# Top-32 search over 56 candidates in place of four full passes, with a per-row proof and a fallback branch

## The chip, the cores and the metric

The kernel runs on one core of one Trainium2 chip. The metric is the device time of one execution in microseconds. An execution consists of the span, from the first to the last instruction of the program, and of a little under 2 us around it. The numbers of the trace come from one profiled execution of the kernel before.

## The reference

Three layers stand behind one another. The first is an attention that keeps, in each row of 576 scores, those that are at least as large as the 32nd largest. The other two are a feed-forward layer and a mixture of eight experts.

```python
batch, n_heads, seq, head_dim = (4, 8, 576, 64)
scores = scale * np.matmul(q, k.transpose(0, 1, 3, 2))
kth = np.partition(scores, -32, axis=-1)[..., -32:-31]
scores = np.where(scores >= kth, scores, -1000000000.0)
scores = scores - np.max(scores, axis=-1, keepdims=True)
attn = np.exp(scores)
attn = attn / (np.sum(attn, axis=-1, keepdims=True) + 1e-09)
x = np.matmul(attn, v)                    # to 2304 tokens x 512
h = np.maximum(x @ w_in, 0.0)             # 512 x 2048
x = h * h @ w_out                         # 2048 x 512
# then a softplus-noise gate picks 2 of 8 experts for a token; an expert is
# relu(x @ w1[e]) @ w2[e] with 512 x 1024 and 1024 x 512
```

The attention has 4 x 8 x 576 = 18432 rows of scores, and each needs its largest score and its 32nd largest.

## The kernel before, in words

**Units.** A unit is a pair of heads and 128 query rows. Four full units of 128 rows and one unit of left-over rows cover the 576 rows of a pair; in the left-over unit the 64 last rows of two heads share the 128 partitions. So there are 144 tiles of 128 x 576 scores, two in a full unit and one in a left-over one.

**One tile.** `scores` (L342) lets TensorE multiply q (split in two parts for precision, L314) by k into `ps`, ScalarE copies `ps` to `sb` (L350), and VectorE searches: four times `max` gives the eight largest of what is left (L355), and three times `match_replace` writes a very small number over these eight (L357). The four groups of eight stand in `m`; the first is the row's largest, the last the 32nd. `softmax` (L361) lets GpSimd multiply the two by constants into `bs` (L363), ScalarE make a large penalty for scores below the 32nd (L364), GpSimd subtract it (L365), and ScalarE take the exponential with the row sum (L366). TensorE then transposes the tile (L376), ScalarE copies it (L378), GpSimd and TensorE handle the last 64 keys (L397 to L406), TensorE multiplies by v (L413), and VectorE divides by the row sum (L385, L389).

**The rest.** The feed-forward layer takes chunks of three token tiles as soon as all heads of these tokens are done; its matmuls stand at L266 to L268 and L280 to L282, its activations at L286 to L290. Before it can run, its weights are converted once from 64-bit to 32-bit numbers and split (`convert`, L134 to L151); two such conversions go with each unit, so they fall into the first part of the span. `route` (L162) picks the experts and scatters tokens to `xs`. The experts (L499) follow at the end. A last part that handles experts with more than 640 tokens stands behind a branch (L833, L834), which these inputs do not take.

**What sets the order.** Each engine runs its own queue in order. The program hands the units out in a fixed interleaving: unit i+2 starts while unit i-1 is finished, and between their steps `step` (L577) puts a fixed allowance of feed-forward work (`RATE`, `FILLS`), at lower priority. A planner then orders the instructions of every engine by priority and by readiness in its own model of the times, and adds the waits. VectorE's queue therefore holds instructions of two or three searches in turn, and everything small that VectorE does for the conversions and for `route`.

**Storage that the change touches.** `vt` holds v of a batch in five tiles of eight buffers (L330), `sb` has eight buffers, `w` four, `m` and `bs` six each.

The search before:

```python
src = sb
for i in range(4):
    nc.vector.max(m[:, i, :], src)
    if i < 3:
        nc.vector.match_replace(out=w, in_to_replace=m[:, i, :], in_values=src, imm_value=NEG)
        src = w
```

Of the kernel before, what the change touches and what calls it, by code (L numbers as in the profile page):

```python
# [8 lines left out]
F32 = mybir.dt.float32  # L9
F32R = mybir.dt.float32r  # L10
I32 = mybir.dt.int32
U32 = mybir.dt.uint32
BF16 = mybir.dt.bfloat16
AF = mybir.ActivationFunctionType
ALU = mybir.AluOpType
PSUM = bass.MemoryType.PSUM

P = 128
SHAPE = (4, 8, 576, 64)
EPS = 1e-9  # L20
BIG = 2.0 ** 96
NEG = -3.0e38
# [19 lines left out]
def tile_order():  # L42

    B, _, S, _ = SHAPE
    n = S // P
    tiles = []
    for b in range(0, B, 2):
        tiles += [(b, i) for i in range(n)] + [(b + 1, i) for i in range(n)] + [(b, None)]
    return tiles


@with_exitstack
def attention_ffn_moe(ctx: ExitStack, tc: tile.TileContext, q, k, v, w_ffn, w_route, noise, w_exp, out):
    nc = tc.nc
    B, H, S, D = SHAPE
    NT, DM = out.shape
    DFF = w_ffn.shape[0] * P
    E, F = w_exp.shape[0], w_exp.shape[1] * P
    NTT = NT // P
    NF = DFF // P  # L60
# [5 lines left out]
    SCALE = 1.0 / float(D) ** 0.5  # L66
# [5 lines left out]
    ROW = DM + 4  # L72


    wsc = [nc.dram_tensor(f"wsc{f}", (P, 2, 2, DM), F32, kind="Internal").ap() for f in range(NF)]
    xs = nc.dram_tensor("xs", (E * NT, ROW), F32, kind="Internal").ap()


    cpool = ctx.enter_context(tc.tile_pool(name="cpool", bufs=1))
# [11 lines left out]
    nc.vector.tensor_scalar(base, iota_e, float(NT), None, op0=ALU.mult)  # L91
    onesb = cpool.tile([P, P], BF16, name="onesb")
    nc.gpsimd.memset(onesb, 1.0)
    cb = cpool.tile([P, 2], F32, name="cb")
    nc.gpsimd.memset(cb[:, 0:1], -SCALE)
    nc.gpsimd.memset(cb[:, 1:2], BIG)
    tiles = tile_order()
    tok_i = cpool.tile([P, NTT], I32, name="tok_i")
    for t, (b, i) in enumerate(tiles):
# [10 lines left out]
    fpool = ctx.enter_context(tc.tile_pool(name="fpool", bufs=2))  # L110
# [194 lines left out]
    apool = actx.enter_context(tc.tile_pool(name="apool", bufs=2))  # L305
# [2 lines left out]

    K4 = {}
    V = {}  # L310

    def split(eng, hi, lo, src, top):

# [13 lines left out]
    def prep_v(b):  # L327
        V[b] = []
        for c in range(NFULL + 1):
            vt = apool.tile([P, H, D], F32, name="vt", bufs=8)  # L330
            nc.sync.dma_start(vt.rearrange("p h d -> p (h d)"), v[b, c])
            V[b].append(vt)

# [8 lines left out]
    def scores(pairs):  # L342

        ps = ps_s.tile([P, 2, 512], F32, name="ps")
        for i, (st, kt) in enumerate(pairs):
            for n in range(2):
                nc.tensor.matmul(ps[:, n, 0:HS], st, kt[:, n * HS:(n + 1) * HS],  # L347
                                 start=(i == 0), stop=(i == len(pairs) - 1))
        sb = apool.tile([P, S], F32, name="sb", bufs=8)
        nc.scalar.activation(sb.rearrange("p (n s) -> p n s", n=2), ps[:, :, 0:HS], AF.Copy)  # L350
        m = apool.tile([P, 4, 8], F32, name="m", bufs=6)
        w = apool.tile([P, S], F32, name="w", bufs=4)
        src = sb
        for i in range(4):
            nc.vector.max(m[:, i, :], src)  # L355
# [3 lines that stand above are left out]
        return sb, w, m  # L359

    def softmax(sb, w, m, sm):  # L361
        bs = apool.tile([P, 2], F32, name="bs", bufs=6)
        nc.gpsimd.tensor_tensor(bs, m.rearrange("p a b -> p (a b)")[:, 0:32:31], cb, op=ALU.mult)  # L363
        nc.scalar.activation(w, sb, AF.Relu, bias=bs[:, 1:2], scale=-BIG)  # L364
        nc.gpsimd.tensor_tensor(sb, sb, w, op=ALU.subtract)  # L365
        nc.scalar.activation(sb, sb, AF.Exp, bias=bs[:, 0:1], scale=SCALE, accum_out=sm)  # L366

    def recip(sm):
        with tc.high_priority(SOON):
# [38 lines left out]
    def times_v(b, hA, pts, t5):  # L408
        av = ps_a.tile([P, 512], F32, name="pa")
        for c in range(NFULL + 1):  # L410
            for i in range(2):
                rhs = pts[i][:, c * P:(c + 1) * P] if c < NFULL else t5[:, 0, :]
                nc.tensor.matmul(av[i * D:(i + 1) * D, 0:P], V[b][c][:, hA + i, :], rhs,  # L413
                                 start=(c == 0), stop=(c == NFULL))
# [219 lines left out]
    chunks, t = [], 0  # L634
# [105 lines left out]
    ps_m = ctx.enter_context(tc.tile_pool(name="ps_m", bufs=2, space=PSUM))  # L740
# [7 lines left out]
        background.append([expert(e, PARTS[:1], ahead), 0])  # L748
    step(10 ** 6)

    todo_e = [(e, PARTS) for e in range(E)]
    for e in range(EARLY):
        todo_e[e] = (e, PARTS[1:])
# [38 lines left out]
    def beyond(e, row):  # L792
        inside = opool.tile([P, 1], F32, name="inside")
        nc.vector.tensor_tensor(inside, row, base[:, e:e + 1], op=ALU.is_lt)
        nc.vector.tensor_scalar(inside, inside, float(-E * NT), float(E * NT), op0=ALU.mult, op1=ALU.add)
        at = opool.tile([P, 1], I32, name="at")
        nc.vector.tensor_tensor(at, inside, row, op=ALU.add)
        nc.vector.tensor_scalar(row, row, float(P), None, op0=ALU.add)
        xr = mpool.tile([P, ROW], F32, name="mr", bufs=3)
        nc.gpsimd.memset(xr, 0.0)  # L800
        nc.vector.tensor_copy(xr[:, DM + 3:DM + 4].bitcast(I32), far)
        nc.gpsimd.indirect_dma_start(
            out=xr, out_offset=None, in_=xs, in_offset=bass.IndirectOffsetOnAxis(ap=at, axis=0),
            bounds_check=E * NT - 1, oob_is_err=False)
        gi = opool.tile([P, 4], F32, name="gi")
        gate(gi, xr, e)
        cu = mpool.tile([P, DM], F32, name="cur", bufs=6)
        nc.gpsimd.memset(cu, 0.0)
        token = bass.IndirectOffsetOnAxis(ap=gi[:, 3:4].bitcast(I32), axis=0)
        nc.gpsimd.indirect_dma_start(out=cu, out_offset=None, in_=out, in_offset=token,  # L810
                                     bounds_check=NT - 1, oob_is_err=False)
        pt = ps_m.tile([P, DM], F32, name="ph")
        for c in range(NC):
            nc.tensor.transpose(pt[:, c * P:(c + 1) * P], xr[:, c * P:(c + 1) * P], ident)
        xt = opool.tile([P, NC, P], F32, name="xto")
        nc.scalar.copy(xt, pt.rearrange("p (c s) -> p c s", c=NC))
        acc = ps_acc.tile([P, DM], F32, name="acc")
        for f in range(NFE):
            raw = mpool.tile([P, 2, DM], F32, name="raww", bufs=3)
            nc.sync.dma_start(raw, w_exp[e, f])  # L820
            ph = ps_m.tile([P, DM], F32, name="ph")
            for c in range(NC):
                nc.tensor.matmul(ph[:, 0:P], raw[:, 0, c * P:(c + 1) * P], xt[:, c, :],
                                 start=(c == 0), stop=(c == NC - 1))
            ht = opool.tile([P, P], F32, name="hto")
            nc.scalar.activation(ht, ph[:, 0:P], AF.Relu)
            nc.tensor.matmul(acc, ht, raw[:, 1, :], start=(f == 0), stop=(f == NFE - 1))
        y = mpool.tile([P, DM], F32, name="y", bufs=3)
        nc.vector.scalar_tensor_tensor(y, acc, gi[:, 2:3], cu, op0=ALU.mult, op1=ALU.add)
        nc.gpsimd.indirect_dma_start(out=out, out_offset=token, in_=y, in_offset=None,  # L830
                                     bounds_check=NT - 1, oob_is_err=False)

    any_extra = nc.values_load(extra[0:1, E:E + 1], min_val=0, max_val=NT)  # L833
    with tc.If(any_extra > 0):  # L834
        none = mpool.tile([P, ROW], F32, name="mr", bufs=3)
        nc.gpsimd.memset(none, 0.0)
        nc.vector.tensor_copy(none[:, DM + 3:DM + 4].bitcast(I32), far)
        row = opool.tile([P, 1], F32, name="row")
        for e in range(E):
            nc.vector.tensor_scalar(row, first, float(e * NT), None, op0=ALU.add)  # L840
            with tc.For_i(0, (NT - CAP) // P, 1):
                blank(e, row, none)
        for e in range(E):
            nc.vector.tensor_scalar(row, first, float(e * NT), None, op0=ALU.add)
            n_extra = nc.values_load(extra[0:1, e:e + 1], min_val=0, max_val=(NT - CAP + P - 1) // P)
            with tc.For_i(0, n_extra, 1):
                beyond(e, row)


def build(shapes):  # L850
    import concourse.bacc as bacc

    nc = bacc.Bacc("TRN2", target_bir_lowering=False, num_devices=1)
    args = []
    for name, (shape, dt) in shapes.items():
        ap = nc.dram_tensor(name, shape, dt, kind="ExternalInput").ap()
        args.append(ap.bitcast(U32) if dt == mybir.dt.uint64 else ap)
    args.append(nc.dram_tensor("out", (2304, 512), F32, kind="ExternalOutput").ap())
    with tile.TileContext(nc, schedule_with_timeline_sim=True) as tc:
        attention_ffn_moe(tc, *args)  # L860
    return nc


# [57 lines left out]
```

## Time and profile before

| | us |
|---|---|
| runs | 1433.07, 1436.71, 1438.79 |
| median | 1436.71 |
| profiled execution | 1438.54 |
| its span | 1436.8 |
| TensorE matmul busy | 1278.8 |
| VectorE busy | 1028.2 |
| ScalarE busy | 844.5 |
| GpSimd busy | 819.5 |

The mean granted clock of TensorE is 0.943 of full speed. Busy time counts an instruction from its start to its end, and consecutive instructions overlap: on TensorE and VectorE the next one starts before the one ahead has ended, so a share of 95% busy does not say that the engine takes no more work. For that the distance from one start to the next is the better measure, and it is read from a timeline.

### The profile page before, as it was taken

What the parts mean: (1) busy time and instruction counts of PE and PEld (TensorE: products, weight loads), DVE (VectorE), ACT (ScalarE), POOL (GpSimd) and SP (SyncE); (2) the same over time, 40 slices, a digit from 0 to 9 for tenths busy, and PEclk for the clock granted to TensorE, in tenths of its full rate; (3) what the DMA queues carried; (4) which work ended last, traced back from release to release, by engine and by line L of the source; (5) the groups of instructions that cost most, each with busy time, mean ns of one, the idle gap of its engine ahead of it and who ended that gap; (6) DMA issues with size and microseconds to landing.
All of it is one profiled execution on the core that took longest, in us unless ns stands there. A gap on an engine that the chain in (4) does not pass through costs nothing. (4 is left out here: it accounts for less than half of the span.)

```text
span 1436.8 us, 23627 instructions
## 1 busy us (share of the span) xinstructions
PE 1278.8 (89%) x7936; PEld 1091.4 (76%) x7936; DVE 1028.2 (72%) x2204; ACT 844.5 (59%) x1741; POOL 819.5 (57%) x1445
## 2 busy tenths in 40 slices
PE   3666558998999999999999999899889999999996
PEld 2454437876787788778878888788778999999995
DVE  8999999998999999999999821045454444444342
ACT  5677777887876787787786664344343333333331
POOL 5788889886688676767756754504234225133131
PEclk9866658999999999999999999999999999999998
DMA  9974447963465544536514556735654344344241
GB/s 336 368 249 169 161 157 249 334 221 133 133 211 187 172 136 159 198 114 217 202 57 161 193 204 224 269 117 192 202 204 157 114 138 154 112 148 148 88 141 37
DMA packets 85219, 257.32 MB, mean 179 GB/s; under 512 B 10716, under 2 KB 10844, under 8 KB 85088
## 3 DMA queue, kind: packets, MB, share of 16 engines
q1 hardware_dynamic: 75808, 227.32, 46.5%
q0 software_dynamic: 9280, 28.40, 5.5%
q8 instruction: 65, 1.06, 0.3%
q14 instruction: 66, 0.54, 0.1%
HBM read 205.71 MB, written 52.06 MB: 179 GB/s over the span
## 5 line engine op out<-in xcount | busy, mean ns | idle before, releaser
L355 DVE MAX8 m<-w 128x8 f32<-128x576 f32 x432 | 311.5, 745 | 0.8
L365 POOL TENSOR_TENSOR sb<-sb,w 128x576 f32<-128x576 f32 x144 | 206.8, 1437 | 54.9 <-ACT w L364 47.0
L357 DVE MATCH_REPLACE8 w<-m,w 128x576 f32<-128x576 f32 x288 | 212.7, 740 | 0.1
L547 DVE SCALAR_TENSOR_TENSOR ht<-ph,ht 128x384 fp32r<-128x384 f32 (+1 forms) x128 | 62.6, 489 | 183.2 <-ACT ht L546 181.7
L546 ACT ACTIVATE ht<-ph 128x384 fp32r<-128x384 f32 (+1 forms) x128 | 55.7, 435 | 220.3 <-PE ph L542 201.5
L562 POOL DMA_INDIRECT out<-y,info x40 | 44.5, 1113 | 244.4 <-DVE y L561 235.4
L347 PE MATMUL ps<-K,qt 128*128 128x288 f32 x640 | 137.3, 345 | 29.6 <-ACT sb L350 13.6
L541 PE MATMUL ph<-xe,wi 128*128 128x384 f32 (+1 forms) x512 | 159.6, 312 | 1.9 <-DVE xe L492 1.9
L540 PE MATMUL ph<-xe,wi 128*128 128x384 f32 (+1 forms) x512 | 160.0, 313 | 0.1
L542 PE MATMUL ph<-xe,wi 128*128 128x384 f32 (+1 forms) x512 | 159.3, 311 | 0.2 <-DVE wi L534 0.2
L347 PEld LDWEIGHTS ps<-K,qt 128*128 128x128 f32 x640 | 104.3, 216 | 46.8 <-ACT sb L350 21.0
L521 PE MATMUL acc<-wo,ht 128*128 128x512 f32 x320 | 127.6, 402 | 3.8 <-ACT ht L546 3.6
L366 ACT ACTIVATE sb<-sb,bs 128x576 f32<-128x576 f32 x144 | 111.8, 776 | 30.7 <-POOL sb L365 30.2
L522 PE MATMUL acc<-wo,ht 128*128 128x512 f32 x320 | 126.4, 397 | 0.0
L376 PE MATMUL pa<-ident,sb 128*128 128x128 f32 x576 | 99.8, 300 | 29.4 <-ACT sb L366 20.4
L290 POOL TENSOR_TENSOR gt<-r,gt 128x384 fp32r<-128x384 f32 x96 | 98.6, 1029 | 44.8 <-ACT gt L289 35.2
L364 ACT ACTIVATE w<-sb,bs 128x576 f32<-128x576 f32 x144 | 110.9, 774 | 21.4 <-POOL bs L363 21.2
L280 PE MATMUL pf<-xT,wi 128*128 128x384 f32 x320 | 113.4, 354 | 10.9 <-ACT xT L390 5.0
L266 PE MATMUL acc<-wo,gt 128*128 128x512 f32 x288 | 114.1, 406 | 7.2 <-DMA wo<-wsc 4.6
L355 DVE MAX8 m<-sb 128x8 f32<-128x576 f32 x144 | 107.4, 746 | 7.8 <-ACT sb L350 6.1
L281 PE MATMUL pf<-xT,wi 128*128 128x384 f32 x320 | 110.2, 345 | 1.3 <-POOL xT L391 1.3
L378 ACT COPY pt<-pa 128x512 f32<-128x512 f32 x144 | 83.4, 579 | 47.5 <-PE pa L376 37.7
(169 smaller groups left out, 3351.2 us busy)
## 6 DMA issues: line engine op xcount, KB each, us to landing
wi<-wsc SPq DMA_DIRECT2D x96, 512.0 KB
wo<-wsc SPq DMA_DIRECT2D x96, 512.0 KB
raww<-in_exp SPq DMA_DIRECT2D x80, 512.0 KB
raw<-in_ffn SPq DMA_DIRECT2D x32, 512.0 KB
wsc<-csp SPq DMA_DIRECT2D x32, 512.0 KB
xs<-xr SPq DMA_DIRECT2D x40, 258.0 KB
mr<-xs SPq DMA_DIRECT2D x40, 258.0 KB
qn<-in_q SPq DMA_DIRECT2D x40, 256.0 KB
```

Of the source, the lines that this page charges most:

```text
L266: nc.tensor.matmul(acc[tt], gt[:, 0, sl], wo[:, 0, :], start=(f == 0), stop=False)
L280: nc.tensor.matmul(ph[:, 0:n], wi[:, 0, sl], xT[:, 0, c, 0:n], start=(c == 0), stop=False)
L347: nc.tensor.matmul(ps[:, n, 0:HS], st, kt[:, n * HS:(n + 1) * HS], start=(i == 0), stop=(i == len(pairs) - 1))
L355: nc.vector.max(m[:, i, :], src)
L357: nc.vector.match_replace(out=w, in_to_replace=m[:, i, :], in_values=src, imm_value=NEG)
L365: nc.gpsimd.tensor_tensor(sb, sb, w, op=ALU.subtract)
L366: nc.scalar.activation(sb, sb, AF.Exp, bias=bs[:, 0:1], scale=SCALE, accum_out=sm)
L521: nc.tensor.matmul(acc[t], hs[i][:, 0, sl], wo[:, 0, :], start=(f == 0), stop=False)
L522: nc.tensor.matmul(acc[t], hs[i][:, 0, sl], wo[:, 1, :], start=False, stop=False)
L540: nc.tensor.matmul(ph[:, 0:n], wi[:, 0, sl], xe[i][:, 0, c, :], start=(c == 0), stop=False)
L541: nc.tensor.matmul(ph[:, 0:n], wi[:, 0, sl], xe[i][:, 1, c, :], start=False, stop=False)
L542: nc.tensor.matmul(ph[:, 0:n], wi[:, 1, sl], xe[i][:, 0, c, :], start=False, stop=(c == NC - 1))
```

## The change

The row of 576 is cut in six parts of 96. For each part the search takes the eight largest and writes the small number over them in `w`. One `max` over the whole of `w` then gives the eight largest of everything that is left. These 48 and 8 stand together in `m`, and the 32nd largest of the 56 is searched in four rounds over 56 columns. If the smallest of the eight in the rest is not larger than the 32nd that was found, nothing outside the 56 can belong to the 32 largest. Otherwise the row could be wrong.

GpSimd's multiplication now makes three columns instead of two (the eighth of the rest and the 32nd, both times the same constant, and the largest), and writes them to one tile `keep` that holds all 144 x 3 columns until the end. Behind the feed-forward layer VectorE compares the two columns for all rows, reduces, and TensorE sums over partitions; after the experts every engine loads the sum, and if it is not zero a branch runs the whole function again with the full search, into scratch of its own. `vt` gets seven buffers instead of eight.

```diff
-    cb = cpool.tile([P, 2], F32, name="cb")
-    nc.gpsimd.memset(cb[:, 0:1], -SCALE)
-    nc.gpsimd.memset(cb[:, 1:2], BIG)
+    cb = cpool.tile([P, 4], F32, name="cb")
+    nc.gpsimd.memset(cb[:, 3:4], BIG)
+    nc.gpsimd.memset(cb[:, 0:2], BIG)
+    nc.gpsimd.memset(cb[:, 2:3], -SCALE)
...
-            vt = apool.tile([P, H, D], F32, name="vt", bufs=8)
+            vt = apool.tile([P, H, D], F32, name="vt", bufs=7)
...
+        w = apool.tile([P, S], F32, name="w", bufs=4)
+        if keep is not None:
+            m = apool.tile([P, 65], F32, name="m", bufs=6)
+            cand = apool.tile([P, 56], F32, name="cand")
+            for i in range(SEGS):
+                sl = slice(i * SEG, (i + 1) * SEG)
+                top = m[:, 8 + 8 * i:16 + 8 * i]
+                nc.vector.max(top, sb[:, sl])
+                nc.vector.match_replace(out=w[:, sl], in_to_replace=top, in_values=sb[:, sl], imm_value=NEG)
+            nc.vector.max(m[:, 0:8], w)
+            src = m[:, 0:56]
+            for i, at in enumerate((57, 8, 16, 25)):
+                nc.vector.max(m[:, at:at + 8], src)
+                if i < 3:
+                    nc.vector.match_replace(out=cand, in_to_replace=m[:, at:at + 8], in_values=src, imm_value=NEG)
+                    src = cand
+            return sb, w, m
...
+        if keep is not None:
+            bs = keep[:, searched[0], :]
+            searched[0] += 1
+            nc.gpsimd.tensor_tensor(bs, m[:, 7:58:25], cb[:, 0:3], op=ALU.mult)
...
+    missed = None
+    if keep is not None:
+        n_rows = keep.shape[1]
+        late = fpool.tile([P, n_rows], F32, name="late", bufs=1)
+        nc.vector.tensor_tensor(late, keep[:, :, 0], keep[:, :, 1], op=ALU.is_gt)
+        worst = fpool.tile([P, 1], F32, name="worst", bufs=1)
+        nc.vector.reduce_max(out=worst, in_=late, axis=mybir.AxisListType.X)
+        worst_b = fpool.tile([P, E], BF16, name="worst_b", bufs=1)
+        nc.vector.tensor_copy(worst_b, worst.to_broadcast([P, E]))
+        total = ps_m.tile([P, DM], F32, name="ph")
+        nc.tensor.matmul(total[:, 0:E], onesb, worst_b, start=True, stop=True)
+        missed = keep.rearrange("p r t -> p (r t)")[:, 0:E].bitcast(I32)
+        nc.vector.tensor_copy(missed, total[:, 0:E])
...
+        keep = kpool.tile([P, n_rows, 3], F32, name="keep")
+        missed = attention_ffn_moe(tc, *args, keep=keep)
+
+        again = nc.values_load(missed[0:1, 0:1], min_val=0, max_val=P)
+        with tc.If(again > 0):
+            attention_ffn_moe(tc, *args)
```

## Rows read from the trace of the kernel before

**Rows 1.** Stretches: us, busy time (instructions) of each engine, granted clock, DMA share, GB/s
```profile
0.00:250.00 250.00, 150.00 (x811) 112.00 (x811) 240.21 (x494) 175.80 (x336) 200.50 (x268) 0.75 0.69 241
250.00:820.00 570.00, 541.61 (x3810) 457.30 (x3810) 546.40 (x1251) 443.43 (x954) 416.96 (x737) 0.99 0.52 178
...
1000.00:1437.00 437.00, 414.95 (x2349) 371.87 (x2347) 188.04 (x316) 139.78 (x278) 126.23 (x275) 0.98 0.41 138
```
**Rows 2.** VectorE's groups by form: count, busy us, mean ns of one, idle before
```profile
L355 DVE MAX8 m<-sb 128x8 f32<-128x576 f32 x144 | 107.4, 746 | 7.8 <-ACT sb L350 6.1 <-POOL bs L363 1.5
...
L357 DVE MATCH_REPLACE8 w<-m,w 128x576 f32<-128x576 f32 x288 | 212.7, 740 | 0.1
...
L201 DVE MAX8 rs<-rs 128x8 f32<-128x8 f32 x18 | 1.7, 151 | 0.0
```
**Rows 3.** Timeline of VectorE, searches in turn (start us, duration us)
```profile
635.38 0.28 DVE L201 MAX8 rs<-rs 128x8 f32<-128x8 f32 x3
635.58 0.74 DVE L355 MAX8 m<-w 128x8 f32<-128x576 f32 x1
636.24 0.07 DVE L357 MATCH_VALUE_LOAD w<-m,sb 128x8 f32 x1
636.30 0.74 DVE L357 MATCH_REPLACE8 w<-m,sb 128x576 f32<-128x576 f32 x1
636.96 0.08 DVE L357 MATCH_VALUE_LOAD w<-m,w 128x8 f32 x1
```
**Rows 4.** Timeline of VectorE, the first search, which is alone there
```profile
7.81 0.76 DVE L355 MAX8 m<-sb 128x8 f32<-128x576 f32 x1
8.60 0.09 DVE L357 MATCH_VALUE_LOAD w<-m,sb 128x8 f32 x1
8.68 0.74 DVE L357 MATCH_REPLACE8 w<-m,sb 128x576 f32<-128x576 f32 x1
9.46 0.76 DVE L355 MAX8 m<-w 128x8 f32<-128x576 f32 x1
```
**Rows 5.** TensorE's groups between 250 and 820 us
```profile
L280 PE MATMUL pf<-xT,wi 128*128 128x384 f32 x284 | 99.3, 350 | 4.6 <-ACT r L286 2.2 <-DMA wi<-wsc 1.5 <-ACT xt L171 0.8
...
L347 PE MATMUL ps<-K,qt 128*128 128x288 f32 x456 | 86.5, 315 | 2.5 <-ACT sb L350 2.4
L266 PE MATMUL acc<-wo,gt 128*128 128x512 f32 x210 | 82.6, 407 | 5.1 <-DMA wo<-wsc 3.7 <-ACT r L288 0.5 <-ACT r L286 0.5
...
L376 PE MATMUL pa<-ident,sb 128*128 128x128 f32 x408 | 64.9, 282 | 4.7 <-ACT pt L378 1.7 <-DVE x L385 1.6 <-DVE x L389 0.7
L413 PE MATMUL pa<-pt,vt 128*64 128x128 f32 x928 | 63.7, 279 | 3.7 <-ACT pt L378 3.5
```
**Rows 6.** Timeline of TensorE, a stretch without a gap
```profile
270.29 0.77 PE L347 MATMUL ps<-K,qt 128*128 128x288 f32 x4
270.90 0.86 PE L268 MATMUL acc<-wo,gt 128*128 128x512 f32 x3
271.60 0.33 PE L280 MATMUL pf<-xT,wi 128*128 128x384 f32 x1
...
273.79 1.09 PE L413 MATMUL pa<-pt,vt 128*64 128x128 f32 x16
274.72 0.39 PE L413 MATMUL pa<-t,vt 128*64 128x128 f32 x4
275.04 0.66 PE L376 MATMUL pa<-ident,sb 128*128 128x128 f32 x4
275.45 0.77 PE L347 MATMUL ps<-K,qt 128*128 128x288 f32 x4
```
**Rows 7.** GpSimd's group of L363 between 0 and 250 us
```profile
L363 POOL TENSOR_TENSOR bs<-m,cb 128x2 f32<-128x2 f32 x38 | 9.5, 252 | 12.4 <-DVE m L355 10.3 <-DVE sm L371 1.9
```
**Rows 8.** GpSimd's load ahead of the last branch (duration ns min/median/max, first and last start)
```profile
L833 POOLq TENSOR_LOAD <-extra x1: 507/507/507, 1430.6 to 1430.6; - x1
```
**Rows 9.** The branch of L834 on the queue that loads TensorE's weights
```profile
L834 PEldq COMPARE_BRANCH  x1: 3590/3590/3590, 1421.7 to 1421.7; - x1
```

More of the change, by code (lines that the diff above doesn't have):

```diff
@@ L52, in attention_ffn_moe @@
 @with_exitstack
-def attention_ffn_moe(ctx: ExitStack, tc: tile.TileContext, q, k, v, w_ffn, w_route, noise, w_exp, out):
+def attention_ffn_moe(ctx: ExitStack, tc: tile.TileContext, q, k, v, w_ffn, w_route, noise, w_exp, out,
+                      keep=None):
     nc = tc.nc
@@ L72, in attention_ffn_moe @@
     ROW = DM + 4
-    wsc = [nc.dram_tensor(f"wsc{f}", (P, 2, 2, DM), F32, kind="Internal").ap() for f in range(NF)]
-    xs = nc.dram_tensor("xs", (E * NT, ROW), F32, kind="Internal").ap()
+    tag = "" if keep is not None else "x"
+    wsc = [nc.dram_tensor(f"wsc{tag}{f}", (P, 2, 2, DM), F32, kind="Internal").ap() for f in range(NF)]
+    xs = nc.dram_tensor(f"xs{tag}", (E * NT, ROW), F32, kind="Internal").ap()
     cpool = ctx.enter_context(tc.tile_pool(name="cpool", bufs=1))
@@ L310, in attention_ffn_moe @@
     V = {}
+    SEGS = 6
+    SEG = S // SEGS
+    searched = [0]
     def split(eng, hi, lo, src, top):
@@ L350, in scores @@
         nc.scalar.activation(sb.rearrange("p (n s) -> p n s", n=2), ps[:, :, 0:HS], AF.Copy)
+        w = apool.tile([P, S], F32, name="w", bufs=4)
[15 more added lines that the diff above has]
+            return sb, w, m
         m = apool.tile([P, 4, 8], F32, name="m", bufs=6)
-        w = apool.tile([P, S], F32, name="w", bufs=4)
         src = sb
@@ L361, in softmax @@
     def softmax(sb, w, m, sm):
-        bs = apool.tile([P, 2], F32, name="bs", bufs=6)
-        nc.gpsimd.tensor_tensor(bs, m.rearrange("p a b -> p (a b)")[:, 0:32:31], cb, op=ALU.mult)
+        if keep is not None:
+            bs = keep[:, searched[0], :]
+            searched[0] += 1
+            nc.gpsimd.tensor_tensor(bs, m[:, 7:58:25], cb[:, 0:3], op=ALU.mult)
+        else:
+            bs = apool.tile([P, 2], F32, name="bs", bufs=6)
+            nc.gpsimd.tensor_tensor(bs, m.rearrange("p a b -> p (a b)")[:, 0:32:31], cb[:, 2:4], op=ALU.mult)
         nc.scalar.activation(w, sb, AF.Relu, bias=bs[:, 1:2], scale=-BIG)
         nc.gpsimd.tensor_tensor(sb, sb, w, op=ALU.subtract)
-        nc.scalar.activation(sb, sb, AF.Exp, bias=bs[:, 0:1], scale=SCALE, accum_out=sm)
+        nc.scalar.activation(sb, sb, AF.Exp, bias=bs[:, 2:3] if keep is not None else bs[:, 0:1], scale=SCALE,
+                             accum_out=sm)
     def recip(sm):
@@ L847, in attention_ffn_moe @@
                 beyond(e, row)
+    return missed
 def build(shapes):
@@ L858, in build @@
     args.append(nc.dram_tensor("out", (2304, 512), F32, kind="ExternalOutput").ap())
-    with tile.TileContext(nc, schedule_with_timeline_sim=True) as tc:
-        attention_ffn_moe(tc, *args)
+    B, H, S, _ = SHAPE
+    n_rows = B * H * (S // P) + B * H // 2
+    with tile.TileContext(nc, schedule_with_timeline_sim=True) as tc, \
+            tc.tile_pool(name="kpool", bufs=1) as kpool:
+        keep = kpool.tile([P, n_rows, 3], F32, name="keep")
[3 more added lines that the diff above has]
+            attention_ffn_moe(tc, *args)
     return nc
```

## The prediction

> **What bounds the kernel now.** I read the stretches first [rows 1]. Up to 820 us, where the searches run, VectorE is busy 240 of 250 and 546 of 570 us; behind that it is busy 188 of 437 us, and there TensorE leads with 415 of 437. So anything VectorE is spared counts before 820 us only, and the two stretches there have to be taken apart. In the first, the other engines have room: GpSimd 200.5 of 250, ScalarE 176, TensorE 150, the last at a granted clock of 0.75. In the second, TensorE is busy 542 of 570 us at nearly full clock, about as much as VectorE. The question is whether it could take more.
>
> Next come VectorE's groups and its timeline, because "busy" hides the overlap. One `max` over 576 columns lasts 746 ns [rows 2], but the instruction behind it starts 0.66 us after it (635.58 to 636.24), a value load takes 0.06 and a replace 0.66 (636.30 to 636.96) [rows 3]. So one search occupies VectorE for 4 x 0.66 + 3 x (0.06 + 0.66) = 4.80 us, and 144 of them for 691 us. That distance holds where several searches stand in the queue in turn. Where one search is alone each step waits for the one ahead: `max` to value load 0.79 us, replace to next `max` 0.78 [rows 4]. I call the extra 0.13 us a handover. In the crowded queue it is hidden behind another search.
>
> Last, how full TensorE is between 250 and 820 us, by the distance of starts in a stretch without a gap [rows 6]: 0.1525 us for 288 columns (four from 270.29), 0.233 for 512 (three from 270.90), 0.1825 for 384 (twelve from 271.60), 0.058 and 0.08 for the two groups of L413, 0.1025 for a transpose. Times their counts [rows 5]: three lines of 284 at 384 columns 155 us; 456 at 288 columns 70; three lines of 210 or 211 at 512 columns 147; 408 transposes and 114 like them at L399 and L400 53; L413 928 x 0.058 and 228 x 0.08 72; the some 190 left of the stretch's 3810, at about 0.1 as for a transpose, 19. That is 517 of 570 us, so TensorE has 53 us of room and no more.
>
> **The change part by part.**
>
> *The search.* The eight-column `max` of the routing shows the fixed part: three of them take 635.38 to 635.58, 0.067 us each [rows 3]. Against 0.66 at 576 columns that is 1.044 ns a column. So 96 columns cost 0.159 us and 56 columns 0.117. No row shows these widths; I put replace on the same line, as it agrees with `max` at 576. The six parts cost 6 x (0.159 + 0.06 + 0.159) = 2.27 us, the `max` over the rest 0.66, the four rounds 4 x 0.117 + 3 x (0.06 + 0.117) = 1.00. Together 3.93 us, which is 0.87 less than before. The bounds: if all is hidden as now, VectorE is spared 144 x 0.87 = 125 us. There are fourteen handovers in a tile: six inside the parts, one before the wide `max`, one behind it, six in the rounds. If all show, a search costs 3.93 + 14 x 0.13 = 5.75 us, 137 us more than now in all. I take 3.93, nearer to rows 3, because the six parts don't depend on each other and a second search usually stands in the queue; both ends count for the range.
>
> One rule speaks against it. The Trainium skill ("VectorE: DVE Perf Modes", section "Rules for kernel authors") says to keep the number of instructions low, since each drains the pipe before the next one starts. Here 10 instructions become 29. Charged with whole durations (746 ns at 576 and 151 at 8 columns in rows 2, so 243 and 201 at 96 and 56), a search would cost 6 x (243 + 70 + 243) + 746 + 4 x 201 + 3 x (70 + 201) = 5.70 us, much like the case with all handovers. Rows 3 disagree for neighbours that don't depend on each other, where 0.66 us passes and not 0.746; rows 4 agree for those that do. It is among the rivals below.
>
> *The first 250 us.* 38 searches reach L363 there [rows 7], so VectorE is spared 38 x 0.87 = 33 us. At the other end stands nothing, if GpSimd takes its place at once. GpSimd's 200.5 us fit into 217, at 92%, a little tighter than a queue that also waits on ScalarE keeps up. I take 25 us.
>
> *250 to 820 us.* The other 106 searches spare 92 us of VectorE, but TensorE cannot shrink below 517. So the gain lies between 0 (TensorE's present 542 of 570 busy is all it can do in this mixture) and 53 us. The expert stage shows 415 of 437 busy, 95%, with TensorE alone in the lead. I take 30 us, just above the middle: VectorE keeps some 90 us of slack and stops holding TensorE up, but other waits, on ScalarE and GpSimd, stay. What is late next is TensorE.
>
> *`bs` of three columns in `keep`.* The instruction keeps its size class (252 ns at two columns [rows 7]): nothing. All tiles share one buffer now; were each write to wait for the exponential of the tile before, the loop of L363 to L366 would still be shorter than the 5.4 us between two searches (570 / 106), so I cost it at 0 and have no row for it.
>
> *`vt` with seven buffers.* At each of three batch changes one more of five loads waits for the old batch to end. Between nothing and, at worst, one tile's 5.4 us three times; 0, since v is needed only at the end of a unit.
>
> *The proof.* Four short VectorE instructions and one small matmul in a stage where VectorE is idle over half the time [rows 1]. TensorE's part is about 0.1 us, and a `ph` buffer is held until VectorE has copied the sum: +1 us, between 0 and 3.
>
> *The second branch.* It costs each engine one more load, 0.51 us [rows 8], and one more jump, this time over a second copy of the whole program. The jump over the last part took TensorE's weight queue 3.59 us [rows 9]. Between 0.5 and 4.1 us on the path, nothing hides it; I take 4.
>
> **Sum.** -25 - 30 + 1 + 4 = -50 us against the profiled 1438.5 us, which lies 1.8 above the median. Forecast: 1388.5, or 1387 as a median.
>
> **The rivals.**
>
> *Everything is gained.* 33 and 53 us, less 5: 1438.5 - 81 = 1357.5, 1356 as a median. For it: TensorE follows VectorE closely now, and nearly all VectorE time before 820 us is search. Against: GpSimd and TensorE would have to run without a gap.
>
> *TensorE is the bound of the middle already.* Then only the first stretch gains: 1438.5 - 25 + 5 = 1418.5, 1417. For it: 95% busy in both of its stretches. Against: the 53 us of room.
>
> *The handovers show (slower).* The six parts hide each other's, but the wide `max` and the seven steps behind it form one chain, and if the queue has no second search at hand it shows 8 handovers: 3.93 + 1.04 = 4.97 us, 0.17 over the present. VectorE then stays the bound and the time is 1438.5 + 144 x 0.17 + 5 = 1468, 1466. The point from which it decides is 0.87 / 0.13 = 6.7 handovers a tile; near that the time stays the same. With all fourteen it is 1438.5 + 137 + 5 = 1580, and the rule on draining, cited above, ends near there. Against it: the queue of rows 3 shows none.
>
> *The branch is taken.* Then everything runs again with the old search, about 1388 + 1437 = 2825. A row fails when the eighth of the rest is larger than the 32nd found, so when about eight of its 32 largest lie outside the best eight of their parts. I counted this over the reference's 18432 rows: the most in any row is seven. So the branch is not taken, though the margin is one.
>
> **How the numbers follow.** Forecast 47% (its own range 1367 to 1407), everything gained 18%, middle without gain 14%, about six handovers and the same time 7%, handovers 11% and 1% with all of them, branch 2%. Faster by over 0.5% (7 us, about what a measurement of this kernel can tell from no change): 47 + 18 + 14 = 79%. Within it: 7%. Slower: 14%. The range for 8 in 10 takes in the first three cases, with 13 us under the full gain for a TensorE that packs better than my count, and reaches to 1432: 1343 to 1432.
>
> **What would show it.** On VectorE's timeline `max` over 96 columns starts 0.16 us after the one ahead, over 56 columns 0.12; a search takes about 4 us of the queue. The searches end near 765 us, 55 before the 820 at which the second stretch is cut, after a first stretch of about 225. TensorE's busy share between them rises to 97% or more, VectorE's falls by a tenth or more. Behind the searches every stretch keeps its length. I am wrong if instructions of 56 columns stand 0.25 us apart, if the searches end no earlier, or if feed-forward work left over behind the searches takes back what they gained.

## The result, and the profile after

The changed kernel takes 1444.18 us (median of 8 runs, 1439.97 to 1448.48), the kernel before in the same comparison 1437.22 us. The ratio is 1.006, with a 95% interval from 1.0037 to 1.0083. The forecast was 1387 us. Its profiled execution has a span of 1444.6 us against 1436.8, which is 7.8 us more.

The stretches of the changed kernel answer to [rows 1]; the columns are the same.

```profile
0.00:250.00 250.00, 158.19 (x975) 123.48 (x976) 229.68 (x1409) 183.78 (x364) 201.20 (x291) 0.81 0.70 239
250.00:820.00 570.00, 524.06 (x3656) 442.58 (x3655) 481.30 (x3099) 440.81 (x946) 418.04 (x731) 0.97 0.50 171
...
1000.00:1445.00 445.00, 418.71 (x2384) 374.91 (x2382) 191.71 (x323) 143.34 (x283) 128.73 (x279) 0.98 0.43 139
```

VectorE was relieved between 250 and 820 us, from 546 to 481 us, but TensorE did not fill up: it fell from 542 to 524. A finer cut shows where. First the kernel before, then the changed one, in the stretches 0 to 100, 100 to 250, 250 to 420 and 420 to 820 us.

```profile
0.00:100.00 100.00, 52.85 (x284) 39.72 (x284) 93.02 (x190) 65.69 (x119) 68.19 (x103) 0.87 0.94 326
100.00:250.00 150.00, 97.14 (x528) 72.28 (x527) 147.19 (x305) 110.11 (x217) 132.32 (x166) 0.67 0.52 183
250.00:420.00 170.00, 157.70 (x1062) 130.84 (x1062) 161.79 (x353) 135.04 (x288) 133.24 (x213) 0.98 0.61 210
420.00:820.00 400.00, 383.91 (x2750) 326.47 (x2749) 384.61 (x899) 308.39 (x666) 283.72 (x524) 1.00 0.48 164
```
```profile
0.00:100.00 100.00, 46.52 (x287) 36.25 (x289) 86.96 (x543) 66.57 (x122) 65.09 (x104) 0.90 0.92 318
100.00:250.00 150.00, 111.67 (x690) 87.23 (x691) 142.72 (x866) 117.21 (x243) 136.11 (x188) 0.75 0.55 186
250.00:420.00 170.00, 130.67 (x903) 106.75 (x901) 156.71 (x946) 134.26 (x283) 143.52 (x201) 0.89 0.50 172
420.00:820.00 400.00, 393.39 (x2755) 335.82 (x2754) 324.60 (x2154) 306.55 (x664) 274.51 (x530) 1.00 0.51 170
```

TensorE does 8 us more work up to 250 us (15 more between 100 and 250), then 27 less between 250 and 420, where it was busy 158 of 170 us before and is 131 now. Behind 420 us it is busy 393 of 400: it then works off what was not done earlier. GpSimd is the engine that got fuller between 250 and 420 us, 143.5 us against 133.

The granted clock of TensorE falls with the work in that stretch, from 0.98 to 0.89: it is more often at the lower of its two levels (1.2 GHz). At one such place, behind a gap of 3.67 us, three matmuls of 512 columns take 1.54 us, where three took 0.86 in [rows 6]; from 374 to 387 us the granted clock is 0.50. What this costs in all was not separated from the gaps.

```profile
373.81 1.54 PE L273 MATMUL acc<-wo,gt 128*128 128x512 f32 x3 [3.67 <-POOL gt L295]
```

What TensorE lacks is the feed-forward work of the first chunk. The same stretch, for the matmuls into `acc` and into `pf` alone (the feed-forward layer's, with 30 to 40 of the routing), shows it, first before and then after; the first busy time and count are TensorE's:

```profile
250.00:420.00 170.00, 50.99 (x184) 33.84 (x183) 0.00 (x0) 1.56 (x3) 0.98 0.61 210
250.00:420.00 170.00, 55.04 (x288) 47.20 (x289) 0.00 (x0) 12.84 (x28) 0.98 0.61 210
```
```profile
250.00:420.00 170.00, 34.25 (x107) 21.32 (x105) 0.00 (x0) 1.56 (x3) 0.89 0.50 172
250.00:420.00 170.00, 30.20 (x148) 26.24 (x148) 0.00 (x0) 7.15 (x15) 0.89 0.50 172
```

These fall from 472 to 255, while attention's matmuls (into `ps` and `pa`) rise from 590 to 648. Each of the chunk's sixteen steps needs weights that a conversion has stored. The following lines give the shortest, median and longest duration in ns, and the first and the last start in us, each time before and then after. The view of `wsc` has the stores of converted weights:

```profile
L151 SPq DMA_DIRECT2D wsc<-csp x32: 319/326/1365, 45.7 to 329.9; - x32
```
```profile
L156 SPq DMA_DIRECT2D wsc<-csp x32: 319/326/470, 38.4 to 372.8; - x32
```

The view of `sb` has the copies of the scores:

```profile
L350 ACT ACTIVATE sb<-ps x144: 624/652/705, 7.1 to 818.2; 128x576 f32<-128x576 f32 x144
```
```profile
L358 ACT ACTIVATE sb<-ps x144: 623/651/738, 7.1 to 781.7; 128x576 f32<-128x576 f32 x144
```

The view of `gt` has the last activation of each of the 96 feed-forward steps:

```profile
L289 ACT ACTIVATE gt<-r x96: 505/525/550, 226.7 to 932.9; 128x384 fp32r<-128x384 f32 x96
```
```profile
L294 ACT ACTIVATE gt<-r x96: 505/525/562, 208.5 to 940.9; 128x384 fp32r<-128x384 f32 x96
```

So the change did what was hoped of it to the attention: the first feed-forward step comes 18 us earlier and the last scores are copied 36 us earlier. But the last conversion is stored 43 us later, and the feed-forward layer ends 8 us later. The queue that issues transfers shows the last weights going straight from the store to the load (changed kernel, start and duration in us). The load of `wo` for the sixteenth step starts 4.9 us behind the store of these weights; the load of `wi` between them belongs to the second chunk.

```profile
372.83 0.34 SPq L156 DMA_DIRECT2D wsc<-csp  x1
373.28 0.37 SPq L279 DMA_DIRECT2D wi<-wsc  x1
377.69 0.80 SPq L281 DMA_DIRECT2D wo<-wsc  x2
```

The second chunk follows. ScalarE's timeline shows its first step at 362.43 us before and at 406.70 after:

```profile
362.43 0.52 ACT L289 ACTIVATE gt<-r 128x384 fp32r<-128x384 f32 x1
```
```profile
406.70 0.53 ACT L294 ACTIVATE gt<-r 128x384 fp32r<-128x384 f32 x1
```

What stands ahead of the conversions is read from GpSimd's groups up to the last of them, up to 330 us before and up to 373 us after.

```profile
L365 POOL TENSOR_TENSOR sb<-sb,w 128x576 f32<-128x576 f32 x50 | 72.6, 1454 | 9.0 <-ACT w L364 7.9 <-DMA out<-xr 0.9
L150 POOL TENSOR_TENSOR csp<-ca,csp 128x512 fp32r<-128x512 f32 x32 | 42.3, 1323 | 4.6 <-ACT csp L149 4.5
L146 POOL TENSOR_TENSOR ca<-ca,raw 128x512 uint32<-128x512 uint32 x32 | 41.8, 1306 | 2.3 <-DVE ca L144 0.7 <-POOL gt L290 0.7 <-POOL sb L365 0.7
```
```profile
L394 POOL TENSOR_TENSOR sb<-sb,w 128x576 f32<-128x576 f32 x63 | 91.2, 1457 | 6.8 <-ACT w L393 4.6 <-DVE m L366 2.0
L155 POOL TENSOR_TENSOR csp<-ca,csp 128x512 fp32r<-128x512 f32 x32 | 42.7, 1334 | 5.7 <-ACT csp L154 4.5 <-DMA xs<-xr 0.7 <-POOL lf L436 0.4
L151 POOL TENSOR_TENSOR ca<-ca,raw 128x512 uint32<-128x512 uint32 x32 | 41.9, 1311 | 13.9 <-DVE ca L149 8.3 <-issue 2.6 <-POOL sb L394 2.0
```

The conversions cost GpSimd the same 84 us in both. But 63 tiles of attention have passed in front of the last conversion, where 50 had before. The durations of all its instructions until then add up to 320 us instead of 280. That is 40 us more, and the last store is 43 us later. GpSimd is not full in either: without the overlaps it is busy 308 of 373 us, and 271 of 330 before, some 82% both times. So the groups show that more attention goes ahead of the conversions, and not yet what holds a conversion back.

At the other end, the profile shows the price of the second branch. TensorE's last matmuls, before and after:

```profile
1424.28 0.62 PE L523 MATMUL acc<-wo,ht 128*128 128x512 f32 x2
```
```profile
1426.07 0.63 PE L553 MATMUL acc<-wo,ht 128*128 128x512 f32 x2
```

The span ends 11.9 us behind them before and 17.9 us behind them now, 6.0 us more. From the last feed-forward activation to these matmuls the changed kernel takes 6 us less, for a reason that is not shown. So the 7.8 us by which the span is longer are made up of 8 at the end of the feed-forward layer, -6 in the experts and +6 at the end.

### The profile page after: what moved, and what is told of

Its sections match the earlier page's. It is cut to its first block, busy times and chain, and to the rows that moved or that the text cites. A ratio compares the mean times of both kernels' runs of the same rounds, so it can differ in the third digit from the quotient of the medians.

```text
span 1444.6 us, 26379 instructions
## 1 busy us (share of the span) xinstructions
PE 1271.8 (88%) x7937; PEld 1089.4 (75%) x7937; DVE 941.0 (65%) x4944; ACT 844.5 (58%) x1741; POOL 818.4 (57%) x1446
## 5 line engine op out<-in xcount | busy, mean ns | idle before, releaser
L367 DVE MATCH_REPLACE8 w<-m,sb 128x96 f32<-128x96 f32 x864 | 201.3, 242 | 0.0
L366 DVE MAX8 m<-sb 128x8 f32<-128x96 f32 x864 | 167.7, 245 | 31.4 <-ACT sb L358 25.7
L355 PE MATMUL ps<-K,qt 128*128 128x288 f32 x640 | 133.9, 336 | 41.6 <-ACT sb L358 17.2
L393 ACT ACTIVATE w<-sb,keep 128x576 f32<-128x576 f32 x144 | 109.6, 772 | 36.2 <-POOL keep L389 35.3
L395 ACT ACTIVATE sb<-sb,keep 128x576 f32<-128x576 f32 x144 | 111.7, 776 | 22.1 <-POOL sb L394 21.2
L271 PE MATMUL acc<-wo,gt 128*128 128x512 f32 x288 | 117.4, 418 | 5.7 <-DMA wo<-wsc 3.0
L406 PEld LDWEIGHTS pa<-ident,sb 128*128 128x128 f32 x576 | 69.9, 151 | 62.2 <-issue 20.0
L272 PE MATMUL acc<-wo,gt 128*128 128x512 f32 x288 | 112.8, 403 | 0.0
```

Source lines behind the costliest of these rows:

```text
L271: nc.tensor.matmul(acc[tt], gt[:, 0, sl], wo[:, 0, :], start=(f == 0), stop=False)
L366: nc.vector.max(top, sb[:, sl])
L367: nc.vector.match_replace(out=w[:, sl], in_to_replace=top, in_values=sb[:, sl], imm_value=NEG)
L406: nc.tensor.transpose(pt[:, c * P:(c + 1) * P], e[:, c * P:(c + 1) * P], ident)
```

## The experiments

Times are medians in us. The ratio is to the kernel before on the same chip, with its 95% interval. "Last store" is the last store of converted weights in the run's own profile. The runs stand on several chips, where the kernel before takes 1432.7 to 1437.2, so differences between runs are taken from the ratios; 0.1% is 1.4 us.

| run | us | ratio | last store |
|---|---|---|---|
| before | 1432.7 to 1437.2 | 1 | 329.9 |
| after | 1444.18 | 1.006 (1.0037 to 1.0083) | 372.8 |
| after_conv_first | 1440.87 | 1.0064 (1.0047 to 1.0082) | 377.4 |
| before_conv_first | 1442.74 | 1.0066 (1.0045 to 1.0087) | 332.2 |
| after_light_conv | 1413.98 | 0.9867 (0.9839 to 0.9895) | 346.0 |
| before_light_conv | 1443.88 | 1.0086 (1.0056 to 1.0117) | 308.2 |
| after_sub_on_dve | 1430.83 | 0.9976 (0.9961 to 0.9991) | 347.7 |
| before_sub_on_dve | 1471.26 | 1.0252 (1.0235 to 1.0269) | 349.7 |
| after_max_twice | 1453.71 | 1.0141 (1.0124 to 1.0158) | 343.0 |
| after_no_branch | 1432.72 | 0.9984 (0.9972 to 0.9996) | 371.4 |
| after_zeros_spread | 1426.40 | 0.9928 (0.9900 to 0.9956) | 340.7 |
| before_zeros_spread | 1441.80 | 1.0043 (1.0032 to 1.0054) | 304.3 |
| after_zeros_sub | 1425.14 | 0.9928 (0.9900 to 0.9957) | 287.7 |
| after_both_on_dve | 1441.38 | 1.0041 (1.0028 to 1.0055) | 350.3 |
| after_proof_no_if | 1436.89 | 1.0004 (0.9984 to 1.0025) | 371.0 |
| after_zeros_no_branch | 1421.21 | 0.988 (0.984 to 0.992) | 339.8 |

**The planner's priority of the conversions.**

```diff
-CONVERT_LATER = 1000
+CONVERT_LATER = 0
```

> The changed kernel with the weight conversions planned at the priority of the attention around them (CONVERT_LATER 0 in place of 1000), nothing else. Theory C (conversions): in the changed kernel the last conversion is stored at 373 us against 330 before, the feed-forward layer of the first chunk loads each weight right behind its store, and TensorE is short of work between 250 and 410 us. If so, the last store comes before 330 us, the first activation of the second chunk (407 us in the changed kernel, 362 before) falls to 350 or less, and the time to 1400-1425. Rival P (TensorE is full in the middle, so an earlier start only moves its work): 1440-1450, whatever the stores do. Rival H (the search's steps cost more than counted): no change either.

> The kernel before with the same one constant (CONVERT_LATER 0). Theory C: before, the stores come just ahead of the loads for the last three of sixteen weights only, so little is to be had, and attention's first tiles come later by what the conversions take: 1425-1445. Rival P: 1432-1442, no change. It is the control: what this constant does without the new search.

A miss, and no test of the two theories: the stores did not move (377 us, and 332 in the kernel before), so this constant does not decide when a conversion gets through. With it raised, 64 tiles still pass ahead of the last conversion, so the low priority alone is not what holds it back. The kernel before is 0.7% slower with the constant changed, though its last store hardly moved: a changed order of the program alone can be worth 9 us.

**A lighter conversion.**

```diff
-        nc.scalar.activation(lo_w, lo_w, AF.Copy, scale=2.0 ** -29)
-        nc.gpsimd.tensor_tensor(a, a, lo_w, op=ALU.add)
```

> The changed kernel with the low words of the 64-bit weights left out of the conversion, which takes one ScalarE instruction (0.68 us) and one GpSimd instruction (1.3 us) from each of the 32 conversions, 42 us of GpSimd in all; the priority stays low. Theory C: GpSimd is 91% busy between 100 and 250 us, so the conversions end 30 us or more sooner and the time falls to 1405-1425, lower than the kernel before with the same cut by 15 us or more. Rival P: the time falls by under 10 us.

> The kernel before with the same low words left out. Theory C: VectorE bounds the first stretch and the conversions gate only the last weights, so 1422-1436, a gain of 15 us at most and less than in the changed kernel. Rival P: within 5 us of the kernel before. If both kernels gain alike, the conversions are not what sets the two apart.

In the changed kernel the last store comes 27 us earlier and the time falls by 28 us (1.006 to 0.9867), to 1.3% under the kernel before. In the kernel before the same cut brings the last store forward by 22 us, and it is 0.9% slower, where 1422 to 1436 or no change was expected. So the conversions gate the changed kernel and not the one before. Rival P ("under 10 us") falls.

**The subtraction on VectorE.** Now nothing is left out.

```diff
-        nc.gpsimd.tensor_tensor(sp[:, 1, :], val, sp[:, 0, :].bitcast(F32), op=ALU.subtract)
+        nc.vector.tensor_tensor(sp[:, 1, :], val, sp[:, 0, :].bitcast(F32), op=ALU.subtract)
```

> The changed kernel with one of a conversion's two GpSimd instructions, the subtraction at the end (1.32 us, 32 times, 42 us), done by VectorE. Nothing is left out. Theory G (GpSimd queue): up to the last conversion GpSimd works 320 us in the changed kernel and 280 before, because 13 more tiles of attention get through it ahead of that conversion; TensorE then lacks the first chunk's feed-forward work and the backlog stays to the end. If so, the last store comes some 25 us or more earlier than 373, and the time is 1408-1425. Rival P (TensorE's backlog is there in any case): 1438-1448. Rival V (VectorE is still near its limit, and 32 x 0.6 us more on it costs): 1450 or more.

> The kernel before with the same subtraction on VectorE. Theory G: there VectorE is the bound up to 820 us, so 32 x 0.6 us more on it lengthen the stretch of the searches by up to 20 us, while the conversions gate only the last weights: 1432-1455, no gain. If it gains like the changed kernel, the move is good by itself and says nothing of the search.

The last store moved by 25 us as expected, and the time by 12, less than the 20 to 36 expected and little more than the 9 us of a changed order. In the kernel before the move costs 38 us, more than the 20 expected at most. VectorE takes 0.94 us for it (30 us in all, where 0.6 was assumed for each). That fits a kernel bound by VectorE, but the last store comes 20 us later there too (349.7), and the two causes are not separated.

**Both instructions on VectorE** (the addition at L151 as well):

> The changed kernel with both of a conversion's GpSimd instructions on VectorE, so GpSimd is spared 84 us and VectorE works some 40 us more. Theory G with VectorE's slack: the last store at 335 or less and 1415-1428. Rival V: VectorE is near its limit in the first 350 us (busy 230 of 250 us there), attention slows by what the conversions gain, and the time is 1430 or more.

Rival V is right here. Moving the second instruction too takes back most of the gain, and the last store does not come earlier than with one (350.3). It is still 22 us earlier than in the changed kernel, and the time is nearly the same: the last store alone does not give the time. VectorE's slack in the first 350 us is small.

**The wide maximum twice.**

```diff
             nc.vector.max(m[:, 0:8], w)
+            nc.vector.max(m[:, 0:8], w)
```

> The changed kernel with the wide maximum over 576 columns done twice in each search, with the same result, so VectorE works 144 x 0.67 = 96 us more and the search occupies it for 4.6 us, close to the 4.8 of before. Theory G: VectorE is not what sets the end of the changed kernel; attention slows a little, the conversions get through GpSimd sooner: 1436-1448, no change or a small gain. Rival H (the small steps with their handovers hold the kernel up, VectorE is still the bound): 96 us more on the bound, 1500 or more.

The time is 12 us above the changed kernel for 96 us of added VectorE work, a little outside the expected range and far from rival H. With the slower search 51 tiles instead of 63 go ahead of the last conversion, and it is stored 30 us earlier (343.0). This is the nearest to a test that the faster search is what makes the conversions late.

**The zero fill spread out.** The scratch and the output are filled with zeros by 58 transfers, 15 MB, at the start; the DMA engines are 92% busy in the first 100 us of the changed kernel. Here each group waits for the newest attention result, which it multiplies by zero:

```diff
+    def held(fill):
+        nc.gpsimd.tensor_scalar(fill[:, 0:P], newest[0].bitcast(F32), 0.0, 0.0, op0=ALU.mult, op1=ALU.add)
...
         for e in range(E):
+            held(fill)
...
-        side(zeros, 1, ZEROS_LATER)
+        if i > 0:
+            side(zeros, 1, ZEROS_LATER)
```

> The changed kernel with the zero fill of the scratch and of the output spread out: each of its thirteen groups of transfers waits for the attention result of the unit before it (one GpSimd instruction of 128 columns each), where all of them stand in the first 65 us now and the DMA engines are over 90% busy in 0 to 90 us. Theory G: in that time only four of the 64 conversion loads and stores get through and GpSimd is idle a third of it; with the zeros spread the conversions start earlier, the last store comes 10 to 25 us sooner than 373 and the time falls to 1422-1438. Rival D (the DMA load at the start is no bound; what is spread collides with the conversions later): 1440-1455.

> The kernel before with the same spread zeros. Theory G: its end hangs on the attention, which VectorE bounds, and on the feed-forward layer about equally; the conversions come sooner but attention does not: 1426-1440. If it gains 10 us or more, the start was a bound of both kernels.

> Both edits in the changed kernel: spread zeros and the conversion's subtraction on VectorE. Theory G: both shorten the way to the last store, 330 or less, and the time is 1410-1425, under the kernel before. Rival: TensorE's backlog no longer hangs on the conversions, then it is within 5 us of 1431, which the subtraction alone gave.

With the zeros spread the changed kernel takes 1426.4 us, 0.7% under the kernel before, with nothing left out. The store view and the finer stretches of this run answer to those above:

```profile
L164 SPq DMA_DIRECT2D wsc<-csp x32: 319/323/461, 31.7 to 340.7; - x32
```
```profile
0.00:100.00 100.00, 43.01 (x242) 32.71 (x242) 89.26 (x493) 67.45 (x121) 77.08 (x111) 0.89 0.78 258
100.00:250.00 150.00, 108.14 (x692) 83.62 (x693) 138.79 (x865) 118.11 (x241) 134.60 (x189) 0.81 0.76 245
250.00:420.00 170.00, 150.60 (x1036) 124.40 (x1036) 155.16 (x991) 139.94 (x296) 143.52 (x226) 0.95 0.56 186
420.00:820.00 400.00, 391.94 (x2797) 335.22 (x2796) 324.33 (x2171) 307.98 (x666) 284.61 (x532) 1.00 0.52 171
```

GpSimd works 77 us in the first 100 instead of 65, because conversions reach it sooner, the last store comes 32 us earlier, and TensorE has 151 us of work between 250 and 420 instead of 131. In the kernel before the stores also come 26 us earlier, and the time rises by 0.4%. With both edits the last store falls to 287.7 us and the time is the same within a microsecond or two. So a last store still earlier than 340 us brought nothing more. What binds then is not shown: the first feed-forward step comes later with both edits (232.5 us instead of 208.5), which can hide a gain. TensorE is the likely one, busy 392 of 400 us behind 420.

**The price of proof and branch.** One kernel has neither; one keeps the reduction and lacks the load at the end and the branch:

```diff
-        again = nc.values_load(missed[0:1, 0:1], min_val=0, max_val=P)
-        with tc.If(again > 0):
-            attention_ffn_moe(tc, *args)
```

> The changed kernel without the proof's reduction and without the branch and the second copy of the program behind it. Every theory of the search says the same of it: it shows the price of these two, which was put at 5 us (1 and 4). So 1436-1443. A rival that puts the whole difference there: 1433-1437, level with the kernel before.

> The changed kernel with the proof's reduction kept and only the load at the end and the branch with the second copy of the program left out. Without both the time was 1432.7. If the branch at the end carries the price (the span behind TensorE's last matmul is 17.9 us with it and 12.2 without), 1435-1440. If the reduction in the expert stage carries it, 1441-1445.

> The changed kernel with the zeros spread, and without the proof's reduction and the branch. Theory G and the price of the branch are independent, so they add: 1426.4 - 11.5 = 1415, 1411-1419. This is what the search alone is worth once the conversions are not late: some 20 us. If the two overlap, 1420 or more.

Without both, the changed kernel is level with the one before (0.9984), as the rival said: the branch and the proof are worth 11 us, as much as the whole visible loss. With the reduction kept the ratio is 1.0004, so some 8 us belong to the load and the branch (6 in the profile), and some 3 to the reduction, which is not clear of the intervals of about 3 us on either side. With the zeros spread as well, the ratio is 0.988 against 0.9928 with the branch, 7 us less. 1421.2 us lies outside the expected 1411 to 1419 and where an overlap of the two losses was expected, but with intervals of 0.4% on these ratios 7 us cannot be told from 11.

## Why the prediction was wrong

**What bounds it now: right as far as it went.** That VectorE set the pace before 820 us fits the runs: 30 us more work on VectorE went with 38 us in the kernel before (`before_sub_on_dve`, where the conversions came later too), and 96 us with only 12 in the changed one.

**The search: nearly right.** In the changed kernel 96 columns stand 0.16 us apart from one replace to the next value load, and 56 columns 0.12, as computed. This is VectorE's timeline in the changed kernel:

```profile
301.06 0.08 DVE L367 MATCH_VALUE_LOAD w<-m,sb 128x8 f32 x1
301.13 0.24 DVE L367 MATCH_REPLACE8 w<-m,sb 128x96 f32<-128x96 f32 x1
301.29 0.08 DVE L367 MATCH_VALUE_LOAD w<-m,sb 128x8 f32 x1
...
302.33 0.07 DVE L373 MATCH_VALUE_LOAD cand<-m 128x8 f32 x1
302.39 0.20 DVE L373 MATCH_REPLACE8 cand<-m 128x56 f32<-128x56 f32 x1
302.51 1.49 DVE L148 TENSOR_SCALAR ca<-ca 128x512 uint32<-128x512 uint32 x1
```
```profile
308.74 0.09 DVE L373 MATCH_VALUE_LOAD cand<-m,cand 128x8 f32 x1
308.82 0.20 DVE L373 MATCH_REPLACE8 cand<-m,cand 128x56 f32<-128x56 f32 x1
309.06 0.22 DVE L371 MAX8 m<-cand 128x8 f32<-128x56 f32 x1
```

The handover is there too: 0.24 us from a replace to the `max` behind it (308.82 to 309.06) where it is 0.12 without. Counted over the trace, some 330 of them show, 2.3 a tile of the fourteen possible, most in the rounds over 56 columns and around the wide `max`. With these, and with value loads 0.07 us apart, a search occupies VectorE for some 4.3 us by estimate, not 3.93, against 4.80 before. The durations worked out from rows (243 and 201 ns) came out at 242 to 245 and 200 to 208, but as in [rows 3] neighbours start before the end of the one ahead, so charging whole durations would overstate the cost. The Trainium skill ("VectorE: DVE Perf Modes", section "Rules for kernel authors") says to keep the number of instructions low, because each drains; the trace agrees for a `max` that needs the replace ahead of it (0.24 us behind the start of one that takes 0.20), and not for neighbours that don't depend on each other (0.12 us).

**The first 250 us: right for attention (18 us until the first feed-forward step, 25 predicted), wrong for what it meant.** The step said GpSimd would run "a little tighter" and asked no further. GpSimd there serves two customers, the attention and the conversions. With the faster attention 13 more tiles passed ahead of the last conversion, 40 us of GpSimd's durations, and slowing the search again took 12 of them back. By what a conversion loses its place is argued only. It is not the priority constant, which moved nothing. A rival was not tried: a conversion goes through ScalarE, VectorE and GpSimd in turn with a single `csp` buffer, so each of its steps may wait behind attention in one of three queues, whatever its priority.

**250 to 820 us: this is the step that failed.** It took 30 us of gain from TensorE's 53 us of room, as if feed-forward work were always at hand. It was not. The searches did end earlier, by 36 us where 55 was forecast (the last copy of scores), but the feed-forward layer ended 8 us later: 159 us behind that copy instead of 115. That is the prediction's own last sign of being wrong. From the ninth step on, each weight of the first chunk was loaded behind its own store, and TensorE's busy time between 250 and 420 us fell by 27 us. The room was used up working off that backlog. The light conversion, the moved subtraction and the spread zeros, which have nothing to do with the search, each brought the last store forward by 25 to 32 us and the time down by 12 to 28 in the changed kernel; none gained in the kernel before. Of these, 19 and 28 us (zeros and light conversion) are clear of the 9 us that a changed order alone was worth; 12 (the subtraction) hardly is.

**The rival "TensorE is the bound of the middle already" is neither confirmed nor ruled out:** it forecast 1417 us, and with the last store at 340 us or at 288 the time is the same, 1426. With the conversions in time and without the branch the search is worth 1.2% (0.988), not the 3.5% forecast. Why the rest of the searches' 36 us is not gained is not shown.

**The second branch: mis-sized.** 4 us were taken for it and 1 for the proof; measured were 6 (profile) to 8 (ratios) for it, and some 3 for the proof, not clear of noise. The jump alone was foreseen (it took 5.0 us on TensorE's weight queue, 3.6 in [rows 9]). Not foreseen was that GpSimd starts the load for the second branch only behind the end of the first:

```profile
L911 POOLq TENSOR_LOAD <-keep x1: 312/312/312, 1439.0 to 1439.0; - x1
```

The last scatter of results was issued at 1434.23 us, and the load stands 4.8 us behind it. In between, GpSimd's queue stands in the waits at the end of the first branch (L878), up to 1438.5 us. Before, the same waits (L834, up to 1434.6) had no second branch behind them.

**Handovers, `bs`, `vt` and the branch being taken:** 96 us more on VectorE cost 12 us, so handovers do not set the time; the branch was not taken; `keep` and `vt` were not tried by themselves.

**Left open.** Not shown are what makes a conversion lose its place, why the edits that bring the last store forward make the kernel before slower (0.4 and 0.9%), whether the reduction costs anything, and why the experts take 6 us less. Each edit also changes the planner's order of the whole program, and that part was not separated.

## What to carry to other kernels

When work on the bounding engine is cut, look for what else passes through the queues that the faster work fills: it can be pushed back, as the conversions were here by 43 us, and somebody may wait for it. Room on an engine is worth something only while its work is at hand, so ask for each idle stretch which producer must run first. A proof with a fallback costs its load and jump at the very end, behind the waits of the code ahead of it: 6 to 8 us here.

## What the runs showed of the hardware that was not expected

The subtraction of 128 x 512 took VectorE 0.94 us in the stretch of the conversions, where the same shape takes 0.69 us in the expert stage. What lengthens it was not tried. And the DMA engines are 92 to 94% busy in the first 100 us. About half of the bytes, 15 of some 32 MB (318 GB/s), is zero fill, though the first scatter into `xs` starts only at 476 us: spreading it out was worth 19 us to the changed kernel, and the one before was 0.4% slower with it.
